# Half of an output product made by Strassen's algorithm: seven block products for eight in batches 4 to 7

## The chip, the cores and the metric

The kernel runs on one core of a Trainium2 chip. The metric is the time of one execution on the device, in microseconds (us); the number of a kernel is the median of its runs. Engines are named as in the profile: PE (TensorE, matrix products), DVE (VectorE), ACT (ScalarE), POOL (GpSimd), SP (SyncE, which here only issues transfers).

## The reference

```python
def _attn_ref(q, k, v, p):                       # batch 8, 8 heads, 576 tokens, head size 64
    def sm_attn(qq, kk, vv): ...                 # softmax(scale * qq kk^T) vv
    p_packed = sm_attn(p, k, v)                  # 32 packed rows per head
    return sm_attn(q, p_packed, p_packed)
def _moe_ref(x, w_in, w_out):                    # 4608 tokens, 512 -> 2048 -> 512
    h = x @ w_in
    sp = np.maximum(h, 0.0) + np.log1p(np.exp(-np.abs(h)))
    g = h * erf(sp)
    return (g @ w_out).astype(np.float32)
```

The output of the attention, 576 tokens by 512 for each of 8 batches, is x. The two weights come as 64-bit floats, and the kernel turns their bits into 32-bit ones on the chip.

## The kernel before, in words

Products that need full precision are made of three: a 32-bit operand is split into a high part (a cast to the matmul type, tiles named gh, woh, a2h, wph) and the low rest (a subtraction, gl, wol, a2l, wpl), and high times high, low times high and high times low are summed in PSUM.

The work is cut into 128 units: for each batch b of 8 there are 16 slices f of 128 columns of d_ff. Batches 0 and 1 are taken in halves of 8 slices in turn, the others one after another. Before a batch's units, `attention` makes the second softmax (a2h, a2l), and `w_prime` makes four pieces of the first weight multiplied by the packed rows (wph, wpl), so that h = x w_in is made straight from the softmax.

A unit passes these steps:
- `h_unit`: two token halves c of 288, six matmuls 128x288 each into a PSUM bank (tag ps_h, two of them), copied to hs by ACT (line 846) or DVE (line 848).
- `gate_group`, for groups of units: softplus and erf on ACT (lines 799 and 804, each with a table load), a multiplication on DVE (line 809), the cast gh on DVE or ACT (lines 814 and 816) and the subtraction gl on DVE (line 817).
- `o_unit`: four token tiles of 128. For each the gate tile is the stationary operand and a slice of w_out (128x512) the moving one: three matmuls 128x512, summed over 16 slices in one of four PSUM banks (ps_o0 to ps_o3). At the end ACT copies a bank to ob (line 874), and SP sends it.
- `o_rest`: 64 of the 576 tokens are left over. They go through DRAM (`rest`), and for two batches together 48 matmuls 128x512 are made (tiles "or").

All matmuls go through the helper on line 328. w_out is converted once, and both parts of its 16 slices stay in SBUF (tag wo, 33 buffers).

The order is not written out by hand. Each step is put into a `Program` as an operation of one engine with a due time (key), a duration, the tiles it reads and writes and sometimes a second engine that may take it (`also`). `Program.order` plays a list schedule over PE, ACT, DVE, SP and POOL, with the room of each tile tag, and the operations are emitted in the order in which it started them. On the chip each engine then runs its list in that order and waits on semaphores. The numbers of PLAN shift the due times.

Of the kernel before, what the change touches and what calls it, by code (L numbers as in the profile page):

```python
# [32 lines left out]
    "rest": -2.95,  # L33
# [7 lines left out]
    "also": {'gate': 2.71, 'h': 3.26},  # L41
# [16 lines left out]
    "low until": -1.91,  # L58
}


class Buf:

    def __init__(self, tag, name, make):
        self.tag, self.name, self.make, self.tile, self.parts, self.users = tag, name, make, None, {}, []
# [18 lines left out]
class Program:  # L84
# [5 lines left out]
    def __init__(self, room):  # L90
        self.ops, self.room = [], room
# [27 lines left out]
    def order(self):  # L119
# [10 lines left out]
        room, taken = dict(self.room), set()  # L130
        ready = {e: [] for e in ("PE", "ACT", "DVE", "SP", "POOL")}
# [16 lines left out]
        while events:  # L148
# [4 lines left out]
            for op in todo:  # L153
                if not isinstance(op, Op):
                    continue
                for buf in op.used:
                    left[buf] -= 1
                    if not left[buf] and buf.tag:
                        room[buf.tag] += 1
                for nxt in then[op]:  # L160
                    waits[nxt] -= 1
                    if not waits[nxt]:
                        arrive(nxt)
            for engine, line in ready.items():
# [3 lines left out]
                for i, (_, _, op) in enumerate(line):  # L168
                    if op.run == "exp" and state["within"]:
                        continue  # L170
                    need = {}
                    for buf in op.used:
                        if buf.tag and buf not in taken:
                            need[buf.tag] = need.get(buf.tag, 0) + 1
                    if any(room[t] < n or t in held for t, n in need.items()):
# [18 lines left out]
                op.fresh = [buf for buf in op.used if buf.tag and buf not in taken]  # L194
                for buf in op.fresh:
                    taken.add(buf)
                    room[buf.tag] -= 1
# [27 lines left out]
            f"{o.engine} {o.key} needs {[x.name for x in o.used if x.tag and x not in taken]} {o.run}"  # L225
            for line in ready.values() for _, _, o in line) + " | held: " + ", ".join(
                x.name for x in taken if left[x] and x.tag)
# [17 lines left out]
def tile_pack_attention_moe(ctx: ExitStack, tc: tile.TileContext, qT, kT, v, pT, w_in, w_out, out, rest):  # L245
# [19 lines left out]
    pools = {}  # L265
    for name, bufs, space in (("const", 1, None), ("attn", 2, None), ("wo", 2 * NF + 1, None), ("stage", 2, None),
                              ("wp", 3, None), ("tmp", G, None), ("ps_o", 1, 1), ("ps_h", 2, 1), ("ps_m", 1, 1)):
        kind = {"space": bass.MemoryType.PSUM} if space else {}
        pools[name] = ctx.enter_context(tc.tile_pool(name=name, bufs=bufs, **kind))
    TAGS = {"p": ("attn", 1), "kvq": ("attn", 6), "big": ("attn", 2), "rem": ("attn", 1), "ms": ("attn", 1),  # L270
            "m": ("attn", 2), "sm": ("attn", 2), "pt": ("attn", 3), "a2h": ("attn", 2), "a2l": ("attn", 2),
            "mx": ("attn", 1), "wo": ("wo", 2 * NF + 1), "wst": ("stage", 2), "wph": ("wp", 3), "wpl": ("wp", 3),
            "t0": ("tmp", G), "hs": ("tmp", 2 * G), "gh": ("tmp", 3), "gl": ("tmp", 3), "ob": ("tmp", G),
            "ps_m": ("ps_m", 1), "ps_h": ("ps_h", 2), **{f"ps_o{y}": ("ps_o", 1) for y in range(4)}}
    prog = Program({t: n for t, (_, n) in TAGS.items()})
    names = {}

    def buf(tag, shape, name, dtype=F32):
        pool, bufs = TAGS[tag]
        return Buf(tag, name, lambda: pools[pool].tile(shape, dtype, name=name, tag=tag, bufs=bufs))  # L280
# [99 lines left out]
    def load_w_out(sent, key, f):  # L380
# [10 lines left out]
        wo_hi[f], wo_lo[f] = hi, lo  # L391

# [658 lines left out]
```

## Time and profile before

| what | value |
|---|---|
| median of 3 runs | 716.91 us (715.48 to 717.5) |
| span of the profiled execution, first to last instruction | 715.3 us |
| PE busy | 701.7 us (98%) |
| ACT busy | 525.7 us (73%) |
| DVE busy | 429.4 us (60%) |
| moved by DMA | 74.8 MB |

The page's own time of the profiled execution is its span, and it lies 1.6 us under the median. Matmuls overlap: the "mean ns" of one is its length from start to end, not its share of the time. What one matmul costs in a row of them is read from the starts in a timeline.

### The profile page before, as it was taken

What the parts mean: (1) busy time and instruction counts of PE and PEld (TensorE: products, weight loads), DVE (VectorE), ACT (ScalarE), POOL (GpSimd) and SP (SyncE); (2) the same over time, 40 slices, a digit from 0 to 9 for tenths busy, and PEclk for the clock granted to TensorE, in tenths of its full rate; (3) what the DMA queues carried; (4) which work ended last, traced back from release to release, by engine and by line L of the source; (5) the groups of instructions that cost most, each with busy time, mean ns of one, the idle gap of its engine ahead of it and who ended that gap; (6) DMA issues with size and microseconds to landing.
All of it is one profiled execution on the core that took longest, in us unless ns stands there. A gap on an engine that the chain in (4) does not pass through costs nothing.

```text
span 715.3 us, 13318 instructions
## 1 busy us (share of the span) xinstructions
PE 701.7 (98%) x5185; PEld 568.9 (80%) x5185; DVE 429.4 (60%) x720; ACT 525.7 (73%) x834; POOL 8.4 (1%) x14
## 2 busy tenths in 40 slices
PE   7799999999999999999999999999999999999997
PEld 3458877888797888878788788887888788788886
DVE  2999988896954465467653385445764445434520
ACT  3699998997794678868876387875888467687931
POOL 0000000002010000000000000000000000000000
PEclk9999999999999999999999999999999999999999
DMA  9952485556418120161205312043302310021113
GB/s 318 376 169 70 135 248 160 166 161 153 108 24 234 46 73 14 45 218 41 75 13 176 99 36 72 14 154 107 98 13 66 121 29 17 14 73 46 45 48 105
DMA packets 66527, 74.80 MB, mean 105 GB/s; under 512 B 40224, under 2 KB 41504, under 8 KB 66464
## 3 DMA queue, kind: packets, MB, share of 16 engines
q1 hardware_dynamic: 64864, 71.14, 32.4%
q0 software_dynamic: 1152, 2.10, 2.0%
q8 instruction: 40, 0.66, 0.4%
q10 hardware_dynamic: 448, 0.72, 0.3%
q14 instruction: 23, 0.19, 0.1%
HBM read 54.00 MB, written 19.92 MB: 103 GB/s over the span
## 4 chain that ended last, share of the span: by engine, by line
PE 84%; DMA 1%; DVE 1%; issue 0%; ACT 0%; SPq 0%; DVEq 0%
PE o L328 45%; PE h L328 25%; PE or L328 6%; PE wp L328 4%; PE s L328 2%; DMA wi<-w_in 1%; PE p L328 1%; PE t L564 1%; DVE w_in L338 0%; DVE w_in L336 0%; DVE hs L809 0%; PE r L569 0%; DVE m L549 0%; DVE w_in L334 0%; DVE gh L814 0%
## 5 line engine op out<-in xcount | busy, mean ns | idle before, releaser
L328 PE MATMUL o<-woh,gh 128*128 128x512 f32 x504 | 200.4, 398 | 0.0
L328 PE MATMUL o<-woh,gl 128*128 128x512 f32 x504 | 198.3, 393 | 0.0
L328 PE MATMUL o<-wol,gh 128*128 128x512 f32 x504 | 197.2, 391 | 0.0
L328 PE MATMUL h<-a2h,wph 128*128 128x288 f32 x512 | 153.5, 300 | 0.8 <-ACT a2h L648 0.6
L328 PE MATMUL h<-a2l,wph 128*128 128x288 f32 x512 | 150.9, 295 | 0.8 <-DVE a2l L649 0.8
L328 PE MATMUL h<-a2h,wpl 128*128 128x288 f32 x512 | 150.5, 295 | 0.2 <-DVE wpl L787 0.2
L817 DVE TENSOR_TENSOR gl<-hs,gh 128x576 fp32r<-128x576 f32 (+1 forms) x128 | 95.3, 745 | 83.1 <-ACT gh L816 82.2
L846 ACT COPY hs<-h 128x288 f32<-128x288 f32 x189 | 75.1, 400 | 81.6 <-PE h L328 76.8
L328 PEld LDWEIGHTS o<-woh,gh 128*128 128x128 f32 x504 | 94.5, 188 | 26.4 <-issue 13.4
L328 PEld LDWEIGHTS o<-wol,gh 128*128 128x128 f32 x504 | 94.6, 188 | 21.5
L328 PEld LDWEIGHTS h<-a2h,wph 128*128 128x128 f32 x512 | 96.0, 188 | 14.3 <-ACT hs L846 1.9
L328 PEld LDWEIGHTS o<-woh,gl 128*128 128x128 f32 x504 | 94.6, 188 | 12.0
L328 PEld LDWEIGHTS h<-a2l,wph 128*128 128x128 f32 x512 | 96.0, 188 | 10.0 <-DVE a2l L649 1.3
L328 PEld LDWEIGHTS h<-a2h,wpl 128*128 128x128 f32 x512 | 96.0, 188 | 0.7 <-DVE wpl L787 0.4
L809 DVE TENSOR_TENSOR hs<-t,hs 128x576 f32<-128x576 f32 x128 | 92.0, 748 | 7.0 <-ACT t L804 6.7
L799 ACT ACTIVATE t<-hs 128x576 f32<-128x576 f32 x128 | 86.7, 686 | 3.8 <-DVE hs L848 1.5
L804 ACT ACTIVATE t<-t 128x576 f32<-128x576 f32 x128 | 82.1, 681 | 0.4
L816 ACT CAST gh<-hs 128x576 fp32r<-128x576 f32 (+1 forms) x66 | 44.0, 667 | 36.8 <-PE o L328 36.2
L848 DVE COPY hs<-h 128x288 f32<-128x288 f32 x67 | 30.4, 454 | 41.3 <-PE h L328 41.0
L814 DVE CAST gh<-hs 128x576 fp32r<-128x576 f32 (+1 forms) x62 | 28.0, 452 | 42.9 <-PE o L328 42.5
L799 ACT ACT_TABLE_LOAD x37 | 47.5, 1283 | 0.7
L804 ACT ACT_TABLE_LOAD x37 | 47.5, 1283 | 0.7
(96 smaller groups left out, 648.8 us busy)
## 6 DMA issues: line engine op xcount, KB each, us to landing
q<-qT SPq DMA_DIRECT2D x32, 288.0 KB, 4.6
k<-kT SPq DMA_DIRECT2D x30, 288.0 KB, 5.1
v<-v SPq DMA_DIRECT2D x32, 256.0 KB, 4.2
wos<-w_out SPq DMA_DIRECT2D x16, 512.0 KB, 3.7
out<-ob SPq DMA_DIRECT2D x32, 256.0 KB, 2.1
g<-rest SPq DMA_DIRECT2D x16, 512.0 KB, 3.3
wi<-w_in SPq DMA_DIRECT2D x12, 512.0 KB, 4.5
rest<-gh SPq DMA_DIRECT2D x128, 32.0 KB, 1.5
```

Source lines behind the costliest of these rows:

```text
L328: return nc.tensor.matmul(*args, **kw)
L564: return [nc.tensor.transpose(tbanks[x]()[:, (j % 2 * 2 + r) * P:(j % 2 * 2 + r + 1) * P], a[:, r, j * P:(j + 1) * P], ident[:]) for j in ...
L799: done.append(act(n + PLAN["lag"] - PLAN["act"] - 2, S, lambda t=t, hs=hs: nc.scalar.activation(t[:], hs[:], AF.Softplus), (t,), (hs,), ru ...
L804: erfs.append(act(e + PLAN["lag"] - PLAN["act"] - 4 + i, S, lambda t=t: nc.scalar.activation(t[:], t[:], AF.Erf), (t,), (), run="erf", kin ...
L809: dve(key, S, lambda t=t, hs=hs: nc.vector.tensor_tensor(hs[:], t[:], hs[:], op=ALU.mult), (hs,), (t,))
L814: op = dve(key + plain, width, lambda hs=hs, ghi=ghi, some=some: nc.vector.tensor_copy(ghi[:, some], hs[:, some]), (ghi,), (hs,), True)
L816: also("gate", op, "ACT", act_us(width), lambda hs=hs, ghi=ghi, some=some: nc.scalar.copy(ghi[:, some], hs[:, some]))
L817: op = dve(key + plain, width, lambda hs=hs, ghi=ghi, glo=glo, some=some: nc.vector.tensor_tensor(glo[:, some], hs[:, some], ghi[:, some], ...
L846: op = act(n + c / 2 - PLAN["copy"], n1, lambda ps=ps, t0=t0, t1=t1, n1=n1: nc.scalar.copy(hs[:, t0:t1], ps[:, 0:n1]), ((hs, c),), (ps,))
L848: also("h", op, "DVE", dve_us(n1), lambda ps=ps, t0=t0, t1=t1, n1=n1: nc.vector.tensor_copy(hs[:, t0:t1], ps[:, 0:n1]))
```

## The change

Batches 0 to 3 keep their way. In batches 4 to 7 (PLAN "from") the second product is made by Strassen's algorithm in its form with 7 products (Winograd's). The 2048 columns of d_ff are taken as two halves kh of 1024. For each half the gate, transposed, is a 2x2 block matrix of blocks 512 x 288 (two of d_ff, two token halves), the weight one of blocks 512 x 256, and the output, transposed, one of blocks 256 x 288. The leftover tokens need no way of their own there.

- Weights: `combine` makes the four sums of weight blocks on DVE, splits them into high and low parts, and SP writes them to a DRAM array `parts`, with the three plain blocks that the other products use. 8 calls of `combine`, with due times of units 36 to 58. Since w_out came as 64-bit numbers, its 32-bit form is also written to DRAM (`raw`) and read back for the sums.
- `block(n0, b, kh)`: seven products s = 0 to 6, each in two half-steps g of 12 matmuls 128x128 by 128x288: the weight part is the stationary operand and the gate the moving one. For each half-step 512 KB of `parts` are fetched into a tile st (6 buffers), and the operand is split (cast by ACT or DVE, line 1012 or 1013; subtraction by DVE, line 1014). DVE makes 8 sums of gate tiles per block (line 1006; a tile holds two slices of one token half, 128x576). Results leave PSUM by 2 copies (lines 1058, 1059) and 5 additions on DVE (line 1064) into tiles cb (6 buffers).
- The first half's results go out through SP into `out_t`, the second half's are added there by a POOL transfer. For the last block of batch 7 one of them is read back and added in SBUF. The host transposes `out_t`.
- The new tiles lie where the 33 wo and 2 wst buffers were: pool "plain" is closed and pool "fast" opened before their first use, and `Program.order` gives none of them out before all plain ones are done. Gates 8 to 15 of a batch (tiles xb) are among them. On PE, the four h halves of slices 9 and 10 of batch 4 stand between the last matmul of 512 columns and the first product.
- Due times and the second engines' delays in PLAN have other numbers; gate groups of batches 4 to 7 end at every fourth slice.

```diff
+            "wo": ("plain", 2 * NF + 1), "wst": ("plain", 2), "ob": ("tmp", G),
+            "ps_m": ("ps_m", 1), "ps_h": ("ps_h", 2), **{t: ("fast", n) for t, n in PLAN["fast"]}}
+    room = {t: n for t, (_, n) in TAGS.items()}
+    plain = {(t, i) for t, (pool, n) in TAGS.items() if pool == "plain" for i in range(n)}
+    room.update({f"ps_o{y}": 1 for y in range(4)})
+    prog = Program(room, {t: [plain] * n for t, n in PLAN["fast"]})
...
+        if w_out.dtype != F32:
+            raw_sent[f] = [dma(key + PLAN["keep"], P * DM * 4, lambda: nc.sync.dma_start(raw[f], made[:]), (), (made,))]
+        kh, j = f // 8, f % 8
+        for x, t in enumerate((hi, lo)):
+            at = (kh, j % 4 // 2, j % 2, x)
+            if j < 4:
+                parts_sent.setdefault((kh, j % 4 // 2), []).append(dma(keep(f), P * 256 * 4, lambda t=t, at=at: nc.sync.dma_start(
+                    parts[at[0], 0, at[1], :, at[2], at[3], :], t[:, 0:256].bitcast(F32)), (), (t,)))
...
+    def combine(kh, j):
+
+        key = PLAN["gen"][0] + (PLAN["gen"][1] - PLAN["gen"][0]) * (4 * kh + j) / 8
...
+        dve(key, DM, lambda: nc.vector.tensor_tensor(t13[:], r[:, :, n:], r[:, 0, :].rearrange("p (o n) -> p o n", o=2),
+                                                     op=ALU.subtract), (t13,), ((r, 0), (r, 1)))
+        dve(key, n, lambda: nc.vector.tensor_tensor(t24[:, 0, :], r[:, 1, n:], t13[:, 0, :], op=ALU.subtract),
+            ((t24, 0),), ((r, 1), t13))
+        dve(key, n, lambda: nc.vector.tensor_tensor(t24[:, 1, :], r[:, 1, 0:n], t24[:, 0, :], op=ALU.subtract),
+            ((t24, 1),), ((r, 1), (t24, 0)))
...
+            dve(key, DM, lambda hi=hi, t=t: nc.vector.tensor_tensor(t[:].bitcast(F32R), t[:], hi(), op=ALU.subtract),
+                ((t, 0), (t, 1)), ((r, x),))
...
             made = pe(n + c / 2, 0.06 + 0.00256 * n1, lambda c=c, ps=ps, terms=terms, cols=cols, n1=n1: [
                 mm(ps[:, 0:n1], w[:, r, fo:fo + P], cols(a, r), start=(m == 0), stop=(m == 5))
                 for m, (r, w, a) in enumerate(terms)], (ps,), needs + [(t, at) for t in (ahi, alo) for at in (((c, c), (c, 2))[:c + 1] if b in DIRECT else (c,))])
-            op = act(n + c / 2 - PLAN["copy"], n1, lambda ps=ps, t0=t0, t1=t1, n1=n1: nc.scalar.copy(hs[:, t0:t1], ps[:, 0:n1]),
-                     ((hs, c),), (ps,))
...
+        def split(x, key, name):
+            th, tl = ("gh", "gl") if name[-1] == "0" else ("gB", "lB")
+            hi, lo = buf(th, [P, S], f"gh{name}", F32R), buf(tl, [P, S], f"gl{name}", F32R)
+            hi.turn = lo.turn = True
+            op = act(key, S, lambda: nc.scalar.copy(hi[:], x[:]), (hi,), (x,))
+            also("cast", op, "DVE", dve_us(S, True), lambda: nc.vector.tensor_copy(hi[:], x[:]))
+            dve(key, S, lambda: nc.vector.tensor_tensor(lo[:], x[:], hi[:], op=ALU.subtract), (lo,), (x, hi))
+            return hi, lo
...
+        def step(s, o, chain, first, operand):
+            to = chains[chain]
...
+            for g in GS:
+                key = mk(s, g)
+                st = buf("st", [P, 2, 2, DM // 2], f"st{name}_{s}_{g}", F32R)
+                dma(key - PLAN["st lead"], P * 2 * DM * 4, lambda st=st, o=o, g=g: nc.sync.dma_start(
+                    st[:].bitcast(F32), parts[kh, o, g]), (st,), (), after=parts_sent[kh, g])
+                hi, lo = operand(g, key - PLAN["split ahead"])
+                pe(key, 12 * 0.1325, lambda st=st, hi=hi, lo=lo, g=g, to=to: [
+                    mm(to[:, d, 0:HT], st[:, x, y, d * P:(d + 1) * P], a[:, x * HT:(x + 1) * HT],
+                       start=(first and g == 0 and x == 0 and m == 0), stop=(g == 1 and x == 1 and m == 2), skip_group_check=True)
+                    for x in range(2) for d in range(2) for m, (y, a) in enumerate(((0, hi), (0, lo), (1, hi)))],
+                   (to,), (st, hi, lo))
+            return to
...
+        def plus(s, to, x, out=None):
+            out = out or buf("cb", [P, S], f"cb{name}_{s}")
+            dve(mk(s, 1) - PLAN["take"], S, lambda: nc.vector.tensor_tensor(two(out), two(x), to[:, :, 0:HT], op=ALU.add),
+                (out,), (to,) if out is x else (to, x))
+            return out
...
+                dma(mk(s, 1), P * S * 4, lambda: nc.gpsimd.dma_start(dst, two(t), accum_op=ALU.add), (), (t,), "POOL",
+                    after=[written[b, half, c]])
...
+        t = step(0, 0, 0, True, lambda g, k: split(A[0, 0, g], k, f"{name}_0_{g}"))
+        m1 = take(0, t)
...
+        for g in GS:
+            add(mk(1, g) - ahead, S1[g], A[0, 1, g], A[1, 1, g], ALU.add)
+            add(mk(1, g) - ahead, A[0, 1, g], A[0, 0, g], A[0, 1, g], ALU.subtract)
+            add(mk(1, g) - ahead, A[0, 0, g], S1[g], A[0, 0, g], ALU.subtract)
+        t1 = step(1, 5, 1, True, lambda g, k: split(A[0, 0, g], k, f"{name}_1_{g}"))
+        u2 = plus(1, t1, m1)
+        t = step(2, 1, 0, False, lambda g, k: split(A[1, 0, g], k, f"{name}_2_{g}"))
...
+        t1 = step(3, 4, 1, False, lambda g, k: split(A[0, 1, g], k, f"{name}_3_{g}"))
+        u3 = plus(3, t1, m1)
+        t = step(4, 3, 2, True, lambda g, k: split(S1[g], k, f"{name}_4_{g}"))
+        send(4, plus(4, t, u3, u3), 1, 1)
+        t1 = step(5, 6, 1, False, lambda g, k: split(A[1, 1, g], k, f"{name}_5_{g}"))
+        send(5, plus(5, t1, m1, m1), 0, 1)
...
+    ends |= {n + 1 for n, (b, f, _, _) in enumerate(units) if b >= NS and f % 4 == 3}
...
+        if "fast" not in pools and any(TAGS.get(t, ("",))[0] == "fast" for x in new for t in x.tags):
+            first_half.close()
+            open_pool(ctx, "fast", 1)
```

Three places in the order of the program. The first is PE in the middle of batch 5's h. In the names h5_5_0 is batch 5, slice 5, token half 0; o4_0_2 is token tile 2 of batch 4; banks is the PSUM of the products; st4_1_4_1 is batch 4, half 1, product 4, half-step 1. Before:

```order
L328 MATMUL o4_0_1_4424<-woh13_1855,gh4_13_5098 128x512
L328 MATMUL o4_0_1_4424<-woh13_1855,gl4_13_5119 128x512
L328 MATMUL o4_0_1_4424<-wol13_1878,gh4_13_5098 128x512
L328 MATMUL o4_0_2_4478<-woh13_1855,gh4_13_5098 128x512
L328 MATMUL o4_0_2_4478<-woh13_1855,gl4_13_5119 128x512
L328 MATMUL o4_0_2_4478<-wol13_1878,gh4_13_5098 128x512
L328 MATMUL h5_5_0_5205<-a2h5_4843,wph5_1_5092 128x288
L328 MATMUL h5_5_0_5205<-a2l5_4856,wph5_1_5092 128x288
L328 MATMUL h5_5_0_5205<-a2h5_4843,wpl5_1_5107 128x288
```

Now:

```order
L403 MATMUL h5_5_1_5644<-a2h5_5131,wph5_1_5534 128x288
L403 MATMUL h5_5_1_5644<-a2l5_5174,wph5_1_5534 128x288
L403 MATMUL h5_5_1_5644<-a2h5_5131,wpl5_1_5555 128x288
L403 MATMUL banks_79<-gh4_1_4_1_5553,st4_1_4_1_5486 128x288
L403 MATMUL banks_79<-gl4_1_4_1_5569,st4_1_4_1_5486 128x288
```

Between two h halves six matmuls of 512 columns stood; now twelve of 288 stand after every two h halves, and they take their stationary operand from st.

The second place is DVE at the same point (L848, L982: copies of h; L809, L934: gate multiplications; L817, L1014: subtractions; L1006: sums of gate tiles; L1064: additions out of PSUM). Before:

```order
L848 COPY hs5_4_5176<-h5_4_0_5165 128x288
L809 TENSOR_TENSOR hs5_0_4985<-t5_0_5049,hs5_0_4985 128x576
L809 TENSOR_TENSOR hs5_1_5028<-t5_1_5079,hs5_1_5028 128x576
L817 TENSOR_TENSOR gl4_15_5201<-hs4_15_4946,gh4_15_5190 128x576
L809 TENSOR_TENSOR hs5_2_5117<-t5_2_5133,hs5_2_5117 128x576
L809 TENSOR_TENSOR hs5_3_5138<-t5_3_5162,hs5_3_5138 128x576
L848 COPY hs5_5_5220<-h5_5_0_5205 128x288
L817 TENSOR_TENSOR gl5_0_5237<-hs5_0_4985,gh5_0_5232 128x576
L817 TENSOR_TENSOR gl5_1_5274<-hs5_1_5028,gh5_1_5269 128x576
```

Now:

```order
L934 TENSOR_TENSOR x5_4_1_5625<-t5_(5, 1)_5680,x5_4_1_5625 128x576
L934 TENSOR_TENSOR x5_6_0_5691<-t5_(7, 0)_5739,x5_6_0_5691 128x576
L1006 TENSOR_TENSOR s15_0_0_5806<-x5_0_1_5246,x5_4_1_5625 128x576
L982 COPY x5_8_1_5781<-h5_9_1_5798 128x288
L1006 TENSOR_TENSOR x5_0_1_5246<-x5_0_0_5242,x5_0_1_5246 128x576
L934 TENSOR_TENSOR x5_6_1_5708<-t5_(7, 1)_5742,x5_6_1_5708 128x576
L1064 TENSOR_TENSOR cb4_1_1_5509<-cb4_1_1_5509,banks_79 128x576
L1006 TENSOR_TENSOR x5_0_0_5242<-s15_0_0_5806,x5_0_0_5242 128x576
L1006 TENSOR_TENSOR s15_0_1_5853<-x5_2_1_5331,x5_6_1_5708 128x576
L1013 CAST gh5_0_2_0_5864<-x5_4_0_5609 128x576
L1006 TENSOR_TENSOR x5_2_1_5331<-x5_2_0_5313,x5_2_1_5331 128x576
L1014 TENSOR_TENSOR gl5_0_1_0_5880<-x5_0_0_5242,gh5_0_1_0_5855 128x576
```

Sums of gate tiles and additions out of PSUM have come between the gate's multiplications and the subtractions; PE's next half-steps wait for the latter.

The third place is the end of DVE's list, from behind the last gate multiplications on. Before:

```order
L809 TENSOR_TENSOR hs7_15_7373<-t7_15_7399,hs7_15_7373 128x576
L817 TENSOR_TENSOR gl7_12_7436<-hs7_12_7250,gh7_12_7431 128x576
L817 TENSOR_TENSOR gl7_13_7454<-hs7_13_7294,gh7_13_7449 128x576
L817 TENSOR_TENSOR gl7_14_7473<-hs7_14_7333,gh7_14_7467 128x576
L817 TENSOR_TENSOR gl7_15_7501<-hs7_15_7373,gh7_15_7495 128x576
L915 TENSOR_TENSOR obr3_7571<-or30_7579,obr3_7571 128x256
L915 TENSOR_TENSOR obr3_7571<-or31_7589,obr3_7571 128x256
```

Now (16 more instructions follow these):

```order
L1014 TENSOR_TENSOR gl7_1_2_0_8338<-x7_12_0_8081,gh7_1_2_0_8335 128x576
L1064 TENSOR_TENSOR cb7_0_0_8032<-cb7_0_0_8032,banks_79 128x576
L1014 TENSOR_TENSOR gl7_1_0_1_8357<-x7_10_0_7975,gh7_1_0_1_8352 128x576
L1064 TENSOR_TENSOR cb7_0_1_8095<-cb7_0_1_8095,banks_79 128x576
L1006 TENSOR_TENSOR s17_1_1_8375<-x7_10_1_8000,x7_14_1_8228 128x576
L1006 TENSOR_TENSOR x7_8_0_7853<-x7_12_0_8081,x7_8_0_7853 128x576
L1006 TENSOR_TENSOR x7_10_1_8000<-x7_10_0_7975,x7_10_1_8000 128x576
L1014 TENSOR_TENSOR gl7_1_3_0_8396<-x7_8_1_7883,gh7_1_3_0_8393 128x576
L1006 TENSOR_TENSOR x7_10_0_7975<-s17_1_1_8375,x7_10_0_7975 128x576
L1014 TENSOR_TENSOR gl7_1_4_0_8415<-s17_1_0_8248,gh7_1_4_0_8412 128x576
L1059 COPY cb7_1_0_8421<-banks_79 128x576
L1014 TENSOR_TENSOR gl7_1_1_1_8425<-x7_10_0_7975,gh7_1_1_1_8417 128x576
```

Before, one subtraction per slice stood between the last gate and the last matmuls; now the sums of the last block and their splits do. On PE 19 half-steps of 12 matmuls follow the last h there, the first five of them of half 0.

## Rows read from the trace of the kernel before

**Rows 1.** The page: busy time of each engine, share of the span.

```profile
PE 701.7 (98%) x5185; PEld 568.9 (80%) x5185; DVE 429.4 (60%) x720; ACT 525.7 (73%) x834; POOL 8.4 (1%) x14
```

**Rows 2.** Busy time by stretch: start:end, length, engines, PEclk, DMA share, GB/s.

```profile
404.50:489.30 84.80, 84.80 (x650) 70.16 (x653) 47.58 (x78) 62.83 (x97) 0.00 (x0) 1.00 0.25 72
...
60.00:90.00 30.00, 29.93 (x186) 26.03 (x185) 29.18 (x49) 29.84 (x51) 0.00 (x0) 1.00 0.35 102
```

**Rows 3.** Timeline of PE, batch 5 to 6: start us, us, what.

```profile
581.86 0.29 PE L328 MATMUL h<-a2h,wph 128*128 128x288 f32 x1
...
582.66 0.40 PE L328 MATMUL o<-woh,gh 128*128 128x512 f32 x1
...
583.36 0.29 PE L328 MATMUL h<-a2h,wph 128*128 128x288 f32 x1
```

**Rows 4.** Groups of PE in 404.5 to 489.3: count | busy us, mean ns | idle.

```profile
L328 PE MATMUL o<-woh,gh 128*128 128x512 f32 x69 | 27.5, 399 | 0.0
```

**Rows 5.** The chain that ended last, longest pieces: start us, us, what.

```profile
678.17 11.61 PE o L328 x51
```

**Rows 6.** Groups of PE in 60 to 90 us, one row of each kind.

```profile
L328 PE MATMUL h<-a2h,wph 128*128 128x288 f32 x35 | 10.6, 302 | 0.1
...
L328 PE MATMUL o<-woh,gl 128*128 128x512 f32 x21 | 8.3, 394 | 0.0
...
L328 PE MATMUL wp<-w_in,pt 64*32 64x512 f32 x16 | 1.1, 601 | 0.0
```

**Rows 7.** Timeline of DVE, instructions that follow each other directly.

```profile
133.19 0.75 DVE L817 TENSOR_TENSOR gl<-hs,gh 128x576 fp32r<-128x576 f32 x1
133.86 0.75 DVE L809 TENSOR_TENSOR hs<-t,hs 128x576 f32<-128x576 f32 x1
...
144.84 0.45 DVE L814 CAST gh<-hs 128x576 fp32r<-128x576 f32 x1
145.21 0.42 DVE L334 TENSOR_SCALAR wo<-wo 128x512 uint32<-128x512 uint32 x1
```

**Rows 8.** Groups of DVE in 404.5 to 489.3.

```profile
L817 DVE TENSOR_TENSOR gl<-hs,gh 128x576 fp32r<-128x576 f32 x18 | 13.6, 755 | 15.0 <-ACT gh L816 14.9
...
L848 DVE COPY hs<-h 128x288 f32<-128x288 f32 x10 | 4.6, 455 | 4.8 <-PE h L328 4.7
L814 DVE CAST gh<-hs 128x576 fp32r<-128x576 f32 x8 | 3.7, 457 | 7.1 <-PE o L328 7.0
```

**Rows 9.** Groups of ACT in 404.5 to 489.3.

```profile
L799 ACT ACTIVATE t<-hs 128x576 f32<-128x576 f32 x16 | 10.9, 685 | 0.7 <-DVE hs L848 0.3
...
L846 ACT COPY hs<-h 128x288 f32<-128x288 f32 x22 | 8.7, 397 | 10.2 <-PE h L328 9.3
L816 ACT CAST gh<-hs 128x576 fp32r<-128x576 f32 x10 | 6.7, 672 | 6.5 <-PE o L328 6.5
...
L799 ACT ACT_TABLE_LOAD x4 | 5.1, 1283 | 0.1
...
L874 ACT COPY ob<-o 128x512 f32<-128x512 f32 x4 | 2.2, 584 | 0.4 <-PE o L328 0.3
...
L543 ACT COPY a<-s 128x576 f32<-128x576 f32 x1 | 0.6, 639 | 1.0 <-PE s L328 1.0
```

**Rows 10.** The page: GB/s in 40 slices; issues, KB each, us to landing.

```profile
GB/s 318 376 169 70 135 248 160 166 161 153 108 24 234 46 73 14 45 218 41 75 13 176 99 36 72 14 154 107 98 13 66 121 29 17 14 73 46 45 48 105
...
g<-rest SPq DMA_DIRECT2D x16, 512.0 KB, 3.3
```

**Rows 11.** The chain within 60 to 130 us: two loads of w_in pieces.

```profile
97.00 5.44 DMA wi<-w_in
...
106.71 4.68 DMA wi<-w_in
```

**Rows 12.** Timelines of PE and DVE: the last instruction of each.

```profile
710.65 0.28 PE L328 MATMUL or<-wol,g 128*128 128x256 f32 x1
...
710.97 0.42 DVE L915 TENSOR_TENSOR obr<-or,obr 128x256 f32<-128x256 f32 x1 [0.23 <-PE or L328]
```

More of the change, by code (lines that the diff above doesn't have):

```diff
@@ L32 @@
     "conv": 2.33,
-    "rest": -2.95,
+    "rest": -2.35,
     "ends": (1, 4, 7, 9, 12, 13, 16),
@@ L40 @@
     "first w": (5.69, 0.5, 1.51, 4.05),
-    "also": {'gate': 2.71, 'h': 3.26},
+    "also": {'gate': 4.54, 'h': 1.3, 'cast': 2.54, 'taken': 0.92, 'h fast': 1.36},
     "warm": (1.4, 7.0, 0.5, 1.2),
@@ L58 @@
     "low until": -1.91,
+    "in turn": ('st', 'gh', 'gl', 'gB', 'lB', 'cb'),
+    "fast": (('st', 6), ('xb', 8), ('sb', 4), ('cb', 6), ('gB', 2), ('lB', 2)),
+    "from": 4,
+    "gate": (2.18, 4.6, 5.53),
+    "copy fast": 0.37,
+    "wp fast": 0.81,
+    "steady fast": (-16.26, -8.13, -4.92, -24.25, -8.19, -1.55, 3.85, 2.62, -15.59, 11.64, -1.38, 2.77, 3.63, -1.26),
+    "ml": 2.5,
+    "split ahead": -0.08,
+    "sums ahead": 0.7,
+    "last ahead": 2.92,
+    "take": 0.65,
+    "st lead": -0.1,
+    "keep": 0.52,
+    "keep parts": (36.0, 54.81),
+    "gen": (36, 58.0, 3.83),
 }
@@ L157, in order @@
                     left[buf] -= 1
-                    if not left[buf] and buf.tag:
-                        room[buf.tag] += 1
+                    if not left[buf] and buf.tags:
+                        give(buf)
                 for nxt in then[op]:
@@ L193, in order @@
                         op.engine, _, op.busy, op.emit = op.other
-                op.fresh = [buf for buf in op.used if buf.tag and buf not in taken]
+                op.fresh = [buf for buf in op.used if buf.tags and buf not in taken]
                 for buf in op.fresh:
-                    taken.add(buf)
-                    room[buf.tag] -= 1
+                    take(buf)
                 op.start, busy = now, op.busy
@@ L224, in order @@
         assert len(done) == len(self.ops), "stuck: " + "; ".join(
-            f"{o.engine} {o.key} needs {[x.name for x in o.used if x.tag and x not in taken]} {o.run}"
+            f"{o.engine} {o.key} needs {[x.name for x in o.used if x.tags and x not in taken]} {o.run}"
             for line in ready.values() for _, _, o in line) + " | held: " + ", ".join(
-                x.name for x in taken if left[x] and x.tag)
+                x.name for x in taken if left[x] and x.tags)
         self.end = max(free.values())
@@ L244, in tile_pack_attention_moe @@
 @with_exitstack
-def tile_pack_attention_moe(ctx: ExitStack, tc: tile.TileContext, qT, kT, v, pT, w_in, w_out, out, rest):
+def tile_pack_attention_moe(ctx: ExitStack, tc: tile.TileContext, qT, kT, v, pT, w_in, w_out, out, rest, out_t, parts, raw):
     nc = tc.nc
@@ new lines, in h_unit @@
+            if b >= NS:
+                t0, t1 = f % 2 * HT, f % 2 * HT + HT
+            op = act(n + c / 2 - PLAN["copy" if b < NS else "copy fast"], n1, lambda to=to, ps=ps, t0=t0, t1=t1, n1=n1: nc.scalar.copy(to[:, t0:t1], ps[:, 0:n1]),
+                     ((to, piece),), (ps,))
+            also("h" if b < NS else "h fast", op, "DVE", dve_us(n1), lambda to=to, ps=ps, t0=t0, t1=t1, n1=n1: nc.vector.tensor_copy(to[:, t0:t1], ps[:, 0:n1]))
+            heads.append(made)
+        if b < NS:
+            group.append((hs, b, f, n))
+        elif f % 2:
+            for c in range(2):
+                group.append((xs[b, f // 2, c], b, (f, c), n))
```

231 lines of the change are left out of this document (196 added, 35 removed).

## Prediction, made before the changed kernel was run

> **What bounds the kernel now.** I read the page's engine totals first: PE is busy 98% of the span, ACT 73%, DVE 60% [rows 1]. Overlapping matmuls can hide gaps, so I went to the busy time by stretch. [...] Then the starts in PE's timeline: six h matmuls of 288 columns take 0.80 us (581.86 to 582.66), 0.133 each, and three of 512 columns 0.70 us (582.66 to 583.36), 0.233 each [rows 3]. Where only those of 512 follow each other, 51 take 11.61 us, 0.228 each [rows 5]. So from about 60 us on, PE's list of matmuls is the time, and a change is worth what it takes out of that list, less the waits that it puts in. ACT and DVE matter only where they make PE wait.
>
> **PE in batches 4 to 7.** Out go 16 slices x 4 tiles x 3 = 192 matmuls of 512 columns per batch, and half of the 48 of the leftover tokens, 24: 216 in all (that stretch has three groups of 69, 207, of the one kind [rows 4]; the rest are of the other). In come 2 halves x 7 products x 2 half-steps x 12 = 336 of 288 columns. They have the form of the h matmuls: a 128x128 stationary operand of the same type, loaded each time, and 288 columns. So I price them at 0.133: 44.7 us. The 216 cost 50.3 us at 0.233 and 49.2 at 0.228. That saves 4.5 to 5.6 us per batch. The o matmuls lie mostly between h in batches 4 to 6, mostly by themselves at the end of batch 7: 3 x 5.6 + 4.5 = 21.3, say **-21 us** (bounds -18 and -22.5). A batch would then last 84.8 - 5.4 = 79.4 us.
>
> [...]
>
> **DVE in batches 4 to 7.** Now the price. Per batch the new order has on DVE 28 subtractions (18 in the stretch of before [rows 8]), 16 sums of gate tiles and 10 additions out of PSUM: 36 more instructions of 128x576. Add one copy of 576 out of PSUM and one more h copy; two casts fewer. An instruction of 576 takes 0.75 us alone [rows 8], but the next one starts 0.67 us later (133.19 to 133.86), a cast 0.37 (144.84 to 145.21) [rows 7]. At these spacings the growth is 37 x 0.67 + 0.4 - 0.7 = 24.5 us, at full lengths 37 x 0.75 + 0.46 - 0.91 = 27.3. On 47.6 us that makes 72 to 75 us of 79.4: DVE goes from 56% to **91 to 94%**.
>
> ACT: 22 casts where 10 were, three copies out of PSUM of 576 (0.64, as the like copy of scores), five copies of outputs (0.58) and one h copy fewer, one table load (1.28) fewer: 12 x 0.67 + 1.9 - 2.9 - 0.4 - 1.3 = +5.3 [rows 9], 68 of 79.4 us, 86%.
>
> Does PE stay fed beside so full a DVE? The stretch from 60 to 90 us has DVE busy 29.2 and ACT 29.8 of 30 us [rows 2]. In it PE made 63 matmuls of 512 (three groups of 21), 107 of 288 (35, 36 and 36) and 16 small ones [rows 6]: 63 x 0.233 + 107 x 0.133 + about 1 = 29.9 us of work. So a full DVE alone need not cost PE anything, if its order fits. But there DVE's surplus was conversion work with slack; here each half-step waits on a chain of gate multiplication, sum, difference, cast and subtraction. Bounds: 0, and one late link of 0.75 us for each of the two half-steps in 8 blocks, 12 us. I take the end that the stretch from 60 to 90 us is nearer to, with something for the chain: **+3 us**.
>
> **The hand-over at batch 4.** No st or xb tile is given out before the last matmul of 512 columns has read its weights. Then the two h banks, full since slice 8, wait for copies of about 0.45 us [rows 8] before PE may go on, and the first 512 KB fetch, which cannot start earlier, takes about 3.3 us to land [rows 10]. Cover is four h halves, 3.2 us. Lower bound 0.5 (the copy), upper 4 (two fetches sharing the bandwidth, no cover): **+1.5**. SP's list has the fetches behind the last leftover load, so they are not held by anything later.
>
> **Fetches after that.** One 512 KB fetch per half-step: 28 in 79.4 us. With six buffers a fetch has five half-steps to land, 8 us at the dense end, against 3.3. At the end one is needed every 1.6 us, 328 GB/s; the second slice of the page shows 376 [rows 10]. Cost 0; if fetches fall behind, the last 19 half-steps show it first. The POOL additions go to DRAM, and only the six cb tiles wait for them: 0.
>
> **The first half.** SP gets writes of `raw` and `parts` between the loads of w_in and w_out, each waiting for its conversion while later loads stand behind it. Two such loads, 5.4 and 4.7 us, are on the chain of waits there [rows 11]. Bounds 0 and half of those two again, 5 us: **+1**. The weight sums, 8 x about 4 instructions' worth of 0.75 = 24 us on DVE, fall into batches 2 and 3, where DVE has some 37 us free per batch [rows 2]: 0.
>
> **The end.** After the last h, PE has 19 half-steps of 1.6 us left. The tenth needs the last gate: copy 0.4, two activations of 0.69 each, a load 1.28, an erf and a cast between, 4.4 us on ACT [rows 9], then 13 instructions on DVE up to its subtraction (the last 12 are in the order), 8.7 to 9.8 us: ready 13.1 to 14.2 us after the last h, wanted at 14.4. One of the 13, the copy of the first result, also waits for half-step 8: **+0.5** (bounds 0 and 4, should half-steps 10 to 12 each wait for a full DVE). The tail behind it has the same form as before, a PSUM addition on DVE and a transfer, and there the last matmul ended 4.4 us before the span did [rows 12]: 0.
>
> **Sum**, against the profiled span of 715.3: -21 + 3 + 1.5 + 1 + 0.5 = -15, 700.3 us. The median lies 1.6 us above that span, so I predict **702 us**.
>
> **Rivals.**
> 1. *Late links.* Each block makes PE wait once per half-step pair on DVE's chain. For it: DVE above 90%, in a fixed order. Against: rows 6. Price 12 in place of 3, and 2 more at the end: 713 us.
> 2. *The first half gives way*, SP's new writes holding the w_in loads. For it: the loads are on the chain [rows 11]; against: from 60 to 90 us, where most of the new writes stand, the transfer engines are busy 0.35 of the time [rows 2]. Price 5 to 8 in place of 1: 706 to 709.
> 3. *DVE becomes the bound in batches 4 to 7* (the other side). A batch has 112 DVE instructions; 72 to 75 us are 0.64 to 0.67 each. If each also waited 0.1 us, an assumed value, for the engine before it in the chain, a batch would take 75 + 11 = 86 us. It decides from 84.8 / 112 = 0.76 us per instruction on. A batch then loses 1.2 us, and the other terms add 3: 716.9 + 4.8 + 3 = 725 us. For it: the chains alternate between DVE, ACT and PE; against: the spacing of rows 7.
> 4. *Product matmuls cost more than those of h*, for instance because high and low parts alternate over one stationary operand that is loaded each time. It decides from 49.8 / 336 = 0.148 us each on; at 0.16 a batch loses 4 us, and with the other terms' 6 that gives 716.9 + 16 + 6 = 739. Against: the same alternation in h, at 0.133 [rows 3]. [...]
>
> **How the numbers follow.** What can be told from no change is 0.3%, 2.2 us. Forecast 64%, all of it faster. Late links 14%, of which 10 faster and 4 within 0.3%. First half 8%, faster. DVE as the bound 11%, 3 within and 8 slower. PE prices 3%, slower. Faster 82, same 7, slower 11. With its own bounds the forecast reaches from 696 (all waits at nothing: 716.9 - 21) to 709; the range 696 to 713 adds the second rival and most of the first. Faster cases hold most of the chance, and within them 696 to 709 is the likeliest's own range.
>
> **What would show it.** Starts of the product matmuls 0.133 us apart, and a period of batches 5 and 6 of 79 to 80 us: the PE price. DVE busy 72 to 75 us of that: its count. PE idle there, ahead of product matmuls and released by DVE's line 1014: the late links. One gap of 1 to 2 us before the first product of batch 4, released by a fetch or an h copy. The first h of batch 4 at the same time as before, within 2 us: the first half. It is wrong if the period stays above 83 us, or if products start 0.15 us apart or more.

## The result and the profile after

The changed kernel takes 726.76 us (726.04 to 727.57) against 717.04 for the kernel before (715.48 to 717.5): ratio 1.0142, interval 1.0127 to 1.0156. It is slower by 9.7 us, where 702 us, and no more than 713, had been forecast. The profiled execution has a span of 724.0 us against 715.3. In the experiments the ratio is to executions of the kernel before made beside them, whose medians are 716.2 to 716.8 us. One of the ten executions of the kernel with six Strassen batches took 1679 us and is not in its ratio.

The page's engine totals of the changed kernel, to be read beside [rows 1]:

```profile
PE 691.1 (95%) x5659; PEld 587.7 (81%) x5659; DVE 555.3 (77%) x933; ACT 546.4 (75%) x870; POOL 26.4 (4%) x29
```

PE has less to do and is busy for a smaller share: waits have come in. A batch is seen at the group of 48 wp matmuls that each of them has, in the chain of waits (start us, us, what):

```profile
414.19 1.88 PE wp L403 x48
...
495.72 1.88 PE wp L403 x48
...
577.26 1.88 PE wp L403 x48
```

The same group in the kernel before:

```profile
404.49 1.88 PE wp L328 x48
489.33 1.88 PE wp L328 x48
574.19 1.88 PE wp L328 x48
```

The period is 81.53 us, before it was 84.85. So the batches did become faster, by less than was forecast. Busy times in one such period (columns as in [rows 2]):

```profile
414.19:495.72 81.53, 80.54 (x771) 75.11 (x778) 71.44 (x115) 66.00 (x106) 5.03 (x4) 1.00 0.85 259
```

The waits of PE in the changed kernel, the longest in total (who waited, for whom: us, times, longest us):

```profile
PE banks L403 <- DVE cb L1064: 6.9, 10, 0.8
PE banks L403 <- ACT ob L1136: 4.2, 8, 0.9
PE banks L403 <- ACT cb L1058: 1.8, 2, 1.1
...
PE banks L403 <- DVE cb L1059: 1.4, 2, 1.2
```

All four lines read accumulators out of PSUM: the products' additions and copies (1064, 1058, 1059) and, in the first half, the copies of outputs (1136). Nothing of the kind is among PE's waits in the kernel before, whose longest belongs to a softmax near the start:

```profile
PE wp L328 <- DVE mx L642: 1.7, 1, 1.7
```

A row of waits names less than is lost, since matmuls of a row overlap (0.29 us long, 0.133 from start to start). One of the ten waits for line 1064 in PE's timeline:

```profile
679.88 0.29 PE L403 MATMUL banks<-gh,st 128*128 128x288 f32 x1
681.02 0.40 PE L403 MATMUL banks<-gh,st 128*128 128x288 f32 x1 [0.85 <-DVE cb L1064]
681.26 0.29 PE L403 MATMUL banks<-gl,st 128*128 128x288 f32 x1
```

From 679.88 to 681.26 are 1.38 us for two steps of 0.133, so that 1.11 us are lost where the row names 0.85. Counted from start to start in this way, the 22 waits of the four rows, 14.3 us by name, cost 20.1 us. The largest part of the products' waits lies at the end; here is the chain there, after the last h:

```profile
702.78 5.06 PE banks L403 x36
707.84 0.02 issue
707.86 0.77 DVE cb L1064
708.62 0.04 issue
708.67 1.86 PE banks L403 x12
```

and DVE's timeline in the same stretch:

```profile
703.33 0.76 DVE L1014 TENSOR_TENSOR gl<-x,gh 128x576 fp32r<-128x576 f32 x1 [1.36 <-ACT gh L1012]
707.86 0.75 DVE L1064 TENSOR_TENSOR cb<-cb,banks 128x576 f32<-128x576 f32 x1 [3.77 <-PE banks L403]
```

This is the case in small. PE's 36 matmuls are three half-steps, the last two of them the second half of product 3 and the second half of product 4. The addition at 707.86 takes product 3 out of its two banks. Product 3 was complete 12 matmuls earlier, at about 706.2, and DVE was idle from 704.1 on. Yet the addition starts only when product 4, which is in the other two banks, is complete too. PE's next half-step (product 5, into the banks of product 3) has to wait for it, so that PE stands still for 0.8 us while DVE makes an addition for which it had time from 706.2 on.

Why it waits so is in one line of the change that the diff above leaves out and the prediction did not look at: `banks = pools["ps_o"].tile([P, 4, 512], F32, name="banks")`. Before, the four accumulator banks were four tiles; now they are one, so that an addition may read two banks at once. The program's waits are a semaphore and a count. Following each count back to the instruction that reaches it: 60 matmuls wait for an eviction (a copy or addition out of PSUM) of banks that they do not write, 11 for one of their own; and 16 evictions of products wait for matmuls into the other pair (the 24 in the expectation below is a rougher count). In this program the waits follow the tile, not the banks.

To say where the time went, I count each matmul of the timeline with its usual spacing (0.133 us at 288 columns, 0.2315 at 512, small ones at their means) and call what is left of the time lost. Switching between kinds counts as lost in every kernel (before and after the change a median of 0.32 us from a matmul of 512 columns to the first one of wp, where 0.23 is usual). "Two tiles" is the first experiment below.

| us | before | changed | two tiles |
|---|---|---|---|
| PE's work | 669.8 | 648.1 | 648.1 |
| lost before 395 us | 39.0 | 45.8 | 42.6 |
| lost from 395 to 420 (hand-over) | 0.3 | 1.9 | 2.4 |
| lost from 420 to the last h | 2.0 | 11.3 | 3.4 |
| lost from there to the last matmul | -0.2 | 10.4 | 2.0 |
| after the last matmul | 4.4 | 6.4 | 7.5 |
| span | 715.3 | 724.0 | 706.0 |

Work fell by 21.7 us, and 30.4 us came in. The table is of one execution each (715.48, 726.12 and 708.22 us).

### The profile page after: what moved, and what is told of

Its sections match the earlier page's. It is cut to its first block, busy times and chain, and to the rows that moved or that the text cites. A ratio compares the mean times of both kernels' runs of the same rounds, so it can differ in the third digit from the quotient of the medians.

```text
span 724.0 us, 14638 instructions
## 1 busy us (share of the span) xinstructions
PE 691.1 (95%) x5659; PEld 587.7 (81%) x5659; DVE 555.3 (77%) x933; ACT 546.4 (75%) x870; POOL 26.4 (4%) x29
## 4 chain that ended last, share of the span: by engine, by line
PE 78%; DVE 9%; ACT 8%; DMA 3%; issue 1%; SPq 0%; DVEq 0%; ACTq 0%
PE banks L403 49%; PE h L403 21%; PE wp L403 4%; DVE cb L1064 2%; PE s L403 2%; PE p L403 1%; DVE x L934 1%; DMA w_in<-w_in 1%; DVE gl L1014 1%; ACT ob L1136 1%; DMA v<-v 1%; ACT t L929 1%; ACT t L924 1%; ACT L924 1%; PE t L687 1%
## 5 line engine op out<-in xcount | busy, mean ns | idle before, releaser
L403 PE MATMUL banks<-gh,st 128*128 128x288 f32 x896 | 197.4, 299 | 12.3 <-DVE cb L1064 6.9
L403 PEld LDWEIGHTS banks<-gh,st 128*128 128x128 f32 x896 | 148.7, 188 | 23.9 <-DVE cb L1064 12.7
L403 PE MATMUL banks<-gl,st 128*128 128x288 f32 x448 | 132.3, 295 | 0.0
L403 PE MATMUL banks<-woh,gh 128*128 128x512 f32 x248 | 100.0, 403 | 4.2 <-ACT ob L1136 4.2
L403 PE MATMUL banks<-woh,gl 128*128 128x512 f32 x248 | 97.5, 393 | 0.0
L403 PE MATMUL banks<-wol,gh 128*128 128x512 f32 x248 | 97.0, 391 | 0.0
L403 PEld LDWEIGHTS banks<-gl,st 128*128 128x128 f32 x448 | 84.2, 188 | 0.0
L1014 DVE TENSOR_TENSOR gl<-x,gh 128x576 fp32r<-128x576 f32 x96 | 71.4, 753 | 11.7 <-ACT gh L1012 11.3
L1012 ACT CAST gh<-x 128x576 fp32r<-128x576 f32 x73 | 48.6, 675 | 39.7 <-PE banks L403 36.5
L944 DVE TENSOR_TENSOR gl<-hs,gh 128x576 fp32r<-128x576 f32 (+1 forms) x64 | 46.9, 734 | 24.9 <-ACT gh L943 24.5
L403 PEld LDWEIGHTS banks<-wol,gh 128*128 128x128 f32 x248 | 46.6, 188 | 10.6
L1064 DVE TENSOR_TENSOR cb<-cb,banks 128x576 f32<-128x576 f32 x39 | 29.4, 753 | 26.9 <-PE banks L403 26.4
L934 DVE TENSOR_TENSOR hs<-t,hs 128x576 f32<-128x576 f32 x64 | 46.9, 749 | 1.9 <-ACT t L929 1.6
```

What stands on the lines that cost most here:

```text
L403: return nc.tensor.matmul(*args, **kw)
L944: op = dve(key + plain, width, lambda hs=hs, ghi=ghi, glo=glo, some=some: nc.vector.tensor_tensor(glo[:, some], hs[:, some], ghi[:, some], ...
L1012: op = act(key, S, lambda: nc.scalar.copy(hi[:], x[:]), (hi,), (x,))
L1014: dve(key, S, lambda: nc.vector.tensor_tensor(lo[:], x[:], hi[:], op=ALU.subtract), (lo,), (x, hi))
L1064: dve(mk(s, 1) - PLAN["take"], S, lambda: nc.vector.tensor_tensor(two(out), two(x), to[:, :, 0:HT], op=ALU.add), (out,), (to,) if out is x ...
```

## The experiments

**Two tiles.** Only the tile is split, one for each chain of products:

```
-    banks = pools["ps_o"].tile([P, 4, 512], F32, name="banks")
+    banks = [pools["ps_o"].tile([P, 2, 512], F32, name=f"banks{y}") for y in range(2)]
-            return Buf(tag, name, lambda: banks[:, y:y + len(tag), :])
+            return Buf(tag, name, lambda: banks[y // 2][:, :, :])
-            return Buf(tag, name, lambda: banks[:, y, :])
+            return Buf(tag, name, lambda: banks[y // 2][:, y % 2, :])
```

> The changed kernel with its four accumulator banks as two tiles of two banks, one for each chain of products, in place of one tile of four; the order of every engine stays. Theory A (one tile ties the chains together: 60 matmuls wait for the eviction of a bank that they do not write, and 24 evictions wait for matmuls of other banks, by the waits in the program): the waits of PE on DVE L1064, L1059, ACT L1058 and L1136 (14.3 us in 22 places in the changed kernel's trace) fall below 3 us, with the 0.1 us after each; 709 to 714 us. Theory B (DVE's in-order queue and its load alone make PE wait): these waits stay, 724 to 727 us. Theory C (half and half: the gaps close, but the subtractions behind the evictions are late next): 715 to 721, with PE waiting for L1014 and L1012.

Measured: 706.83 us (705.02 to 708.22), ratio to the kernel before 0.9858 (0.9841 to 0.9876). That is 20 us less than the changed kernel, more than even theory A gave, which counted the waits by name; by starts they came to 20.1 us. The chain of waits shows the same group at

```profile
411.58 1.88 PE wp L403 x48
491.37 1.88 PE wp L403 x48
571.16 1.88 PE wp L403 x48
```

a period of 79.79 us, and in it PE has no gap, while DVE does the same work as before the split:

```profile
411.58:491.37 79.79, 79.79 (x771) 75.04 (x778) 71.26 (x115) 65.84 (x106) 5.03 (x4) 1.00 0.86 264
```

PE's waits on the four lines fall from 14.3 us in 22 places to 1.3 us in two (0.9 for line 1059, near the end, and 0.4 for line 1136). DVE's 89% of a batch therefore did not make PE wait. Theory B falls, and C too: none of PE's waits is for line 1014 or 1012.

**One tile in the kernel before.** The reverse: before's four tiles of one bank are made one tile of four.

```
+    four = pools["ps_o"].tile([P, 4, 512], F32, name="four")
     def buf(tag, shape, name, dtype=F32):
+        if tag.startswith("ps_o"):
+            return Buf(tag, name, lambda y=int(tag[-1]): four[:, y, :])
```

> The kernel before with its four one-bank accumulator tiles merged into one tile of four banks, nothing else. Theory A: 19 matmuls wait for copies of banks that they do not write, at the end of each batch, as the changed kernel's first half shows (8 waits, 4.2 us on ACT L1136 in four batches, plus 0.1 each): 4 to 11 us more than before, 721 to 728 us. Theory B: no change, 716 to 718 us.

Measured: 726.57 us, ratio 1.0148 (1.0132 to 1.0165), 10.3 us more than before. PE's waits in it:

```profile
PE four L331 <- ACT ob L877: 5.2, 11, 0.9
```

By the count used above 9.6 us more are lost; the row names 5.2 of that, and from start to start its 11 waits cost 8.1. So this one line, without any Strassen product, makes the kernel as slow as the change did. The order of the instructions on every engine is the same in both pairs of kernels, so that the tile alone is at work, and the two experiments together show the products themselves to be a gain.

**Strassen in two batches**, with two tiles:

```
-    "from": 4,
+    "from": 6,
```

> The two-tile kernel with Strassen's products in batches 6 and 7 alone. Theory A (each batch gains 84.85 - 79.8 = 5.06 us, the period in the two kernels' traces, and the weight sums, the hand-over, the end and the last transfers cost once, however many batches follow): 706.8 + 2 x 5.06 = 717 us, 714 to 720, no faster than the kernel before. Theory B (the costs come with each batch, not once): about half of the 9.4 us is left, 711 to 713.

Measured: 717.4 us (715.89 to 719.37), ratio 1.0015 (1.0002 to 1.0028). Theory A gave 717. What costs once, in both of these kernels, is 4 x 5.06 - 9.4 = 10.8 us, and the two batches just pay for it.

**Strassen in six batches**, with two tiles; "keep parts" and "gen" place the writes and the sums of the weights by slices:

```
-    "from": 4,
+    "from": 2,
-    "keep parts": (36.0, 54.81),
+    "keep parts": (14.0, 30.0),
-    "gen": (36, 58.0, 3.83),
+    "gen": (14, 30.0, 3.83),
```

> The two-tile kernel with Strassen's products in batches 2 to 7; the sums of w_out and their writes move ahead, to the slices 14 to 30 of the first two batches, where DVE and ACT are busy 52 of 55 us. Theory A (5.06 us per batch, costs once): 706.8 - 10.1 = 697 us, 693 to 700. Theory B (the sums, 24 us on DVE, find no room there and the hand-over moves into batches that are still converting weights): PE waits in the first 240 us grow by 10 us or more, 705 to 725.

Measured: 716.52 us, ratio 1.0009 (0.9995 to 1.0023). The batches after the hand-over have the period forecast:

```profile
341.08 1.88 PE wp L403 x48
420.87 1.88 PE wp L403 x48
```

79.79 us again. But between 150 and 240 us PE waits for the conversion of a w_out slice and for copies of h that stand behind the sums, among others, in DVE's and ACT's lists:

```profile
PE banks L403 <- ACT woh L462: 5.2, 1, 5.2
PE h L403 <- DVE x L982: 3.9, 2, 2.7
PE h L403 <- ACT x L980: 2.7, 2, 2.1
```

Lost by 235 us: 59.6 against 40.4 in the two-tile kernel, 19 us, of which two batches' gain gives back 10. Theory B, with its mechanism, and with a granted clock of 0.67 to 0.83 in three stretches of ten microseconds on top (last section).

**The last accumulating transfer.** In the last block product 5's output is added on DVE to the half that is read back, and sent from SP:

```
-        send(5, plus(5, t1, m1, m1), 0, 1)
+        plus(5, t1, m1, m1)
+        if not final:
+            send(5, m1, 0, 1)
...
+            had5 = buf("sb", [P, S], f"had5{name}")
+            dma(mk(2), P * S * 4, lambda: nc.sync.dma_start(two(had5), dst5), (had5,), (), after=[written[b, 0, 1]])
+            dve(mk(6) - 1.9, S, lambda: nc.vector.tensor_tensor(m1[:], m1[:], had5[:], op=ALU.add), (m1,), (had5,))
+            dma(mk(6), P * S * 4, lambda: nc.sync.dma_start(dst5, two(m1)), (), (m1,))
```

> The two-tile kernel, and in the last block the accumulating transfer that POOL issues last (product 5's output, issued at 699.7 and landed at 704.6 in the two-tile kernel's trace, 2.6 us after SP's and ACT's last) is replaced by a read of the earlier half, an addition on DVE and a plain transfer from SP. Theory A (POOL's transfers follow one another, each issued after the one before has landed, and the last one ends the span): 2 to 3 us less, 704 us. Theory B (the last products and their transfers end the span all the same): within 0.7 us of 706.8.

Measured: 704.74 us (703.08 to 706.01), ratio 0.9838 (0.9819 to 0.9856). The intervals of this and of the two-tile kernel overlap, so that the times alone are weak; the traces are clear. POOL's issues at the end of the two-tile kernel:

```profile
686.14 1.20 POOL L1073 DMA_DIRECT2D out_t<-cb  x1 [38.87 <-ACT cb L1058]
694.59 1.22 POOL L1073 DMA_DIRECT2D out_t<-cb  x1 [7.25 <-DVE gl L1014]
699.72 1.20 POOL L1073 DMA_DIRECT2D out_t<-cb  x1 [3.91 <-DVE cb L1107]
```

and in this one:

```profile
685.20 1.20 POOL L1073 DMA_DIRECT2D out_t<-cb  x1 [36.81 <-DMA st<-parts]
693.48 1.22 POOL L1073 DMA_DIRECT2D out_t<-cb  x1 [7.08 <-issue]
```

The third is gone, SP sends in its place:

```profile
695.82 0.39 SPq L1108 DMA_DIRECT2D out_t<-cb  x1
```

The time after the last matmul falls from 7.5 to 4.6 us, close to the 4.4 of before. This is the fastest version tried, and it beats both kernels: 11.7 us under the kernel before.

**More work for DVE.** One subtraction in two is issued twice, the order stays:

```
+            def low():
+                if name[-1] == "0":
+                    line("DVE", nc.vector.tensor_tensor(lo[:], x[:], hi[:], op=ALU.subtract))
+                return nc.vector.tensor_tensor(lo[:], x[:], hi[:], op=ALU.subtract)
```

> The two-tile kernel with one subtraction in two done twice over (14 more instructions of 128x576 per Strassen batch, the order of all others the same): DVE's work goes from 71.8 to 81.2 us in a batch of 79.8. Theory A (DVE has almost no slack, as the prediction's third rival has it): the period goes to 82 us or more, with PE waiting for DVE's subtractions and evictions, 716 to 725 us. Theory B (the waits hide in slack, or PE's buffers cover them): period under 80.5, 707 to 711.

Measured: 728.36 us, ratio 1.0172 (1.0156 to 1.0188): more than theory A's top. From the first h of one batch to the next:

```profile
440.30:526.40 86.10, 82.43 (x766) 76.69 (x765) 80.74 (x129) 66.23 (x106) 5.03 (x4) 0.98 0.80 242
```

Here the granted clock is 0.98. The next period, from one wp group to the next, has it at 1.00 throughout:

```profile
495.19:580.61 85.42, 80.85 (x764) 75.11 (x763) 80.69 (x129) 66.21 (x106) 5.03 (x4) 1.00 0.78 236
```

So DVE's 9.4 us more make the batch 5.6 us longer, with DVE busy 94% of it. It does not get to 100%, since it waits for PE too (for h 3.1 us and for a product 1.1 in this period). At 89% the two-tile kernel stands, by an estimate from these two points, some 4 us of DVE work per batch short of the point at which DVE decides. The doubled subtraction makes the chain ahead of a half-step longer as well as DVE fuller, and the run does not separate the two. But PE's waits from 420 to 660 us are only in part for what theory A named, the subtractions and evictions (1.0 and 1.5 of 11.2 us); most are for other work in DVE's and ACT's lists:

```profile
PE h L403 <- ACT x L980: 3.9, 2, 2.0
PE h L403 <- DVE wpl L886: 1.6, 2, 0.8
...
PE banks L403 <- DVE cb L1068: 1.5, 1, 1.5
PE banks L403 <- DVE gl L1017: 1.0, 1, 1.0
```

**Without the sums** of the weight blocks: their arithmetic is left out, and the unsummed blocks are written and fetched in their place.

```
-        dve(key, DM, lambda: nc.vector.tensor_tensor(t13[:], r[:, :, n:], ...
...
+                    dst(y), hi()), (), ((r, x),)))
```

> The two-tile kernel without the arithmetic of the weight block sums (24 us on DVE, and their casts): what is fetched for products 3 to 6 is the unsummed blocks of w_out, so those products are not the reference's; all transfers stay. It asks where the 3.6 us go that the two-tile kernel has lost against the kernel before by 395 us (42.6 against 39.0 us of time in which PE does no work that the two share). Theory A (the sums on DVE hold conversions up): the loss by 395 us falls to 40 or less, 703 to 705 us. Theory B (the new writes and reads on SP's queue, or the order around them): it stays within 0.7 us, 706 to 707.5 us.

Measured: 708.36 us (706.46 to 709.14), and 43.8 us lost by 395 us. So leaving out the sums gains nothing there: theory A falls, though the time lies above theory B's range as well. A part of the 3.6 us belongs to the execution and not to the kernel. In the traces of the two-tile kernel and of this one the granted clock is 0.50 for 6.8 us near the start; in the kernel before, the changed one and the one with the last transfer replaced it is 1.00 there. The same stretch in the two-tile kernel and in the one with the last transfer replaced, PEclk third from the right:

```profile
14.50:21.30 6.80, 5.95 (x52) 2.41 (x42) 4.41 (x11) 2.02 (x3) 0.00 (x0) 0.50 1.05 389
...
14.50:21.30 6.80, 5.93 (x67) 2.78 (x60) 4.85 (x12) 2.08 (x4) 0.00 (x0) 1.00 1.05 390
```

Up to 235 us the kernels with the last transfer replaced and with more work for DVE run the same list of matmuls as the two-tile kernel, and lost 0.8 and 2.0 us less than it did. Whether the new writes on SP's queue, the changed order, or the waits that the two tiles still leave between two banks of one tile make what remains is open; it wasn't tried further.

## Why the prediction was wrong

- **PE's price held.** Work fell by 21.7 us, -21 had been forecast. Products start 0.133 us apart, as the timeline of the changed kernel shows:

```profile
410.04 0.29 PE L403 MATMUL banks<-gh,st 128*128 128x288 f32 x1
410.18 0.29 PE L403 MATMUL banks<-gl,st 128*128 128x288 f32 x1
410.31 0.42 PE L403 MATMUL banks<-gh,st 128*128 128x288 f32 x2
410.57 0.29 PE L403 MATMUL banks<-gl,st 128*128 128x288 f32 x1
```

  The fourth rival, which decides from 0.148 us on, is refuted for these matmuls.
- **DVE's and ACT's load held.** 71.4 us of DVE per batch (72 to 75 forecast), 66.0 of ACT (68): a little under. The batch of before that the forecast counts from, in [rows 4] as well, is the first stretch of [rows 2]. The step "Does PE stay fed beside so full a DVE?" gave +3 us, and in the two-tile kernel it is +1.4 from 420 us to the last h. In the changed kernel it is +9.3.
- **The step that failed** is that one, together with "The end" (+0.5, measured +10.6; +2.2 with two tiles): both listed loads and chains on DVE and ACT, and took for granted that a product in one pair of banks runs while the other pair is being emptied, as the four tiles of before allow (none of PE's waits there is for an eviction of them, and as one tile they cost 5.2 us in 11 waits). The change took that away by making them one tile, and PE waited 14.3 us by name, 20.1 by starts, for evictions. The rival "late links" had PE waits in these places too (12 us and 2 more at the end), but from another cause (DVE's chain, released by line 1014), and its sign to look for, 1014, is not who released PE: lines 1064, 1058 and 1059 did. With two tiles that cause is gone and with it the waits.
- **The first half**: +1 (bounds 0 and 5), measured +6.8; +3.6 with two tiles, up to 2 of which change from one execution to the next. The difference of the two is the same tile, by the copies at line 1136 (4.2 us by name). That the sums hide, as forecast, is borne out by the last experiment.
- **The hand-over**: +1.5, measured +1.6. PE waits there for the last leftover load (0.4 us) and an h copy (0.5), not for the first fetch. The time of batch 4's first h, which was to show the first half right or wrong, was no use: the new order moves that matmul.
- **The fetches**: the median is 4.4 us to landing in place of the 3.3 assumed, and six buffers cover it. Cost 0, as forecast, but for one wait of 0.5 us after 640 us in the two-tile kernel.
- **The tail**: 0 forecast ("the same form as before"), measured +2.0, and +3.1 with two tiles. The two have different causes. In the changed kernel the last transfers of SP and ACT end the span, after POOL's; they take longer to land than those of the kernel before and of the two-tile kernel (3.8 to 4.2 us, where those took 1.9 to 2.2 and 2.0 to 2.3). They were issued while POOL's last one was under way; whether that held them up was not tried. With two tiles POOL's last transfer lands 2.6 us after SP's and ACT's, and it is the tail: replacing it took the tail back to 4.6 us. "POOL additions: 0" was wrong at this one place.
- **The third rival**, DVE as the bound, had nearly the right sum (725 us) by the wrong mechanism: with the same load and two tiles PE has no gap in a batch. Its point of decision is near, though, as the experiment with more work shows: a period of 85.4 to 86.1 with 129 DVE instructions in it (115 in the two-tile kernel), where it had 86 for 112. That the sum came out near the measured 726.8 is luck.
- "It is wrong if the period stays above 83 us": it was 81.5, and the time was wrong all the same. A test on the batches alone could not see the first half and the end, where more than half of the 30.4 us lie.
- **The range**: "with its own bounds" the forecast was said to reach 709. The upper bounds given for the terms add up to more: 716.9 - 18 + 12 + 4 + 5 + 4 = 724 us.

With two tiles 706.8 us were measured, against the 702 forecast for a kernel whose accumulators do not tie the products together.

## What to carry to other kernels

Before pricing loads, list for every buffer that two engines share what it was and what it is: a change that merges tiles changes who waits for whom, even if no instruction is added, and here that was worth 20 us of 727. Look in the waits for an engine released by an eviction of something that it does not touch, and for an idle engine whose input has long been complete. A gain per repetition with a price paid once (5.06 us per batch against 10.8) is read best by changing the number of repetitions.

## What the runs showed of the hardware that was not expected

- In the two-tile kernel the accumulating transfers that POOL issued last went out 0.3 us after the one before had landed (landed at 694.28 and 699.40, next issue at 694.59 and 699.72), though the last one's data were complete at 696.2 and the program makes it wait for no transfer but the first half's, which had landed by 690.7. This does not hold for all accumulating transfers of POOL: those that add the second halves of batches 0 and 1 went out while others were under way, as the issues in the same trace show, the first three within 2.4 us:

```profile
175.17 1.92 POOL L1142 DMA_DIRECT2D out<-ob  x2 [173.87 <-ACT ob L1136]
177.55 0.86 POOL L1142 DMA_DIRECT2D out<-ob  x1 [0.46 <-ACT ob L1136]
```

  The transfers of that line took 3.8 to 7.1 us to land. They write rows of 512 numbers, the ones that waited pieces of 288; whether that is the reason is open.
- In the kernel with six Strassen batches the granted clock was 0.97 from 150 to 160 us and 0.69 from 160 to 170, about PE's wait of 5.2 us (156.4 to 161.6), 1.00 in the next ten, and 0.83 and 0.67 from 180 to 200, where PE was idle for 5.95 of 20 us. Stretches of ten microseconds, PEclk third from the right:

```profile
160.00:170.00 10.00, 7.78 (x54) 5.27 (x55) 8.20 (x14) 7.20 (x13) 0.00 (x0) 0.69 0.84 261
...
190.00:200.00 10.00, 7.90 (x26) 6.37 (x26) 6.46 (x12) 4.66 (x9) 0.00 (x0) 0.67 0.59 210
```

  If these are means of 0.50 and 1.00, the two values of the rows in the last experiment, 0.69 is an estimated 6 us at 0.50. Longer matmuls stand in the chain of the kernel with more work for DVE, in the stretch from 440.30 to 526.40, whose clock is 0.98:

```profile
449.60 1.71 PE h L403 x6
451.31 2.47 PE banks L403 x12
...
514.05 0.80 PE h L403 x6
514.85 1.60 PE banks L403 x12
```

  The first two pieces are 0.91 and 0.87 us longer than the last two, 1.8 together; 0.98 is by the same estimate some 3.4 us at 0.50, about twice that. So, by this estimate, a part of the 19 us lost there is not waiting but slower matmuls. In the changed kernel, whose waits are 1.2 us at most after the start, the clock is 1.00 up to the last matmul (in every stretch from 0 to 718 us).
- With two tiles DVE was busy 89% of a batch without a wait of PE; with more work, at 94%, the period grew from 79.8 to 85.4 us.
